# Loading attention's keys on 64 partitions instead of 128, and writing the low parts across

## The chip, the cores and the metric

One Trainium2 chip, one core. The metric is the device time of one execution in microseconds. The profile comes from one execution of its own.

## What is computed

Attention over 4 batches, 8 heads, 576 positions of 64 elements, with a mask by blocks of 64; its output is cut into 2304 tokens of 512, which pass a mixture of four experts and then a last layer with a softmax in it.

```python
scores = scale * np.matmul(q, k.transpose(0, 1, 3, 2))
mask = block_i >= block_j                       # blocks of 64 positions
scores = np.where(mask, scores, -1000000000.0)
attn = softmax(scores)
x = np.matmul(attn, v)                          # as (2304, 512)
for e in range(4):
    out += p[:, e:e + 1] * (np.maximum(x @ w1[e], 0.0) @ w2[e])
h = out @ w_in                                  # then softmax, a layer norm, @ w_out
```

## The kernel before

Tokens go in 18 tiles of 128 (TILES). Three things run woven into each other: attention in 60-odd steps (`step_a` the scores, `step_b` the exponentials, `step_c` the product with the values, `finish` the scaling of the result), the experts (`emit_h`, `emit_o`) for tiles whose attention is done, and the preparation of weights (`w_steps`). After attention the second half of the tokens goes through the last expert phases, and then the last layer (`m2_h`, `m2_o`).

**Products in parts.** A float32 value x is held as a high part, x rounded, and a low part, x less the high part. For the scores the contraction has 64 elements and TensorE has 128 rows, so the keys' tile `ks` holds the high part in partitions 0 to 63 and the low part in 64 to 127. The queries' tiles `qhi` and `qlo` hold their part twice, in both halves. One matmul of `qhi` and one of `qlo` with `ks` (L915, L918) so give all four products.

**How the keys got there.** The input `kT` has the same 64 rows twice, on 128 partitions. `k_load` and `k_far_load` (through `dup`, L781) load all 128 into a tile of the pool `kr`, which has three buffers and holds raw values (`vraw`) too. `parts` (L788) rounds all 128 partitions into `ks` (L793, on POOL in mode "pp") and then, on partitions 64 to 127 alone, writes raw less rounded over it in place (L795). Batch 0 is done in two pieces: `k_near` takes 192 columns from the tile `near`, and the far 384 columns of each of the eight heads come through `k_far_load`. Batches 1 to 3 take 576 columns for each head through `k_load` and `k_prep`, 24 in all.

**Other names.** `wt` is a split weight: POOL (L231) or ACT (L235) writes its high part, DVE (L238) its low part, in four pieces. `stage` is the raw weight. The first expert's w1 and w2 go through POOL. `hl` is a tile of exponentials in two parts; a DMA transpose on SP makes `pT` of it, on which `step_c` waits. `xh` is a tile of attention's result in two parts; a DMA transpose makes `xT`, on which the first expert matmul (`hps`, L375) waits. `hch` is the hidden layer, `ops` the expert's output.

**What sets the order.** All DMAs are issued by SP in one order, each when what it waits for is there, and a later one does not pass it. Every engine runs its instructions in a fixed order, which a scheduler works out ahead of the run from the program and its own estimate of each instruction's time; an edit to one instruction can so move others. The plan's step numbers (`plan`, L1082) say at which attention step a key is prepared, and up to three loads of the pool `kr` are issued ahead.

Of the kernel before, what the change touches and what calls it, by code (L numbers as in the profile page):

```python
# [7 lines left out]
F32 = mybir.dt.float32  # L8
# [6 lines left out]
AF = mybir.ActivationFunctionType  # L15
ALU = mybir.AluOpType
# [3 lines left out]
NB, NH, S, HD = 4, 8, 576, 64  # L20
# [10 lines left out]
NEAR = 192  # L31
# [32 lines left out]
def tile_kernel(  # L64
# [38 lines left out]
    vec, act, gp, sync = nc.vector, nc.scalar, nc.gpsimd, InOrder(nc.sync)  # L103
# [640 lines left out]
    class Attention:  # L744
# [43 lines left out]
        def parts(self, hi, lo, raw, ps, mode):  # L788
# [5 lines left out]
            eng = vec if mode[1] == "d" else gp  # L794
            eng.tensor_tensor(out=lo[ps], in0=raw[ps], in1=hi[ps], op=ALU.subtract)  # L795

        def k_load(self, b, h):
            self.raws["k", b, h] = self.dup([S], kT[:, b, h, :], "kr")

        def k_prep(self, b, h, mode="pp"):  # L800
            ks = self.kp.tile([128, S], F32R, tag="ks", name="ks")
            self.kS[b, h] = ks
            self.parts(ks, ks, self.raws.pop(("k", b, h)), slice(64, 128), mode)

        def k_near(self, p):

# [7 lines left out]

        def k_far_load(self, h):
            c = 0 if h % 2 == 0 else NEAR
            self.raws["far", h] = self.dup([S - NEAR], kT[:, 0, h, c:c + S - NEAR], "kr")

        def k_far(self, h, mode="pp"):
            c = 0 if h % 2 == 0 else NEAR  # L820
            o = self.kS[0, h][:, c:c + S - NEAR]
            self.parts(o, o, self.raws.pop(("far", h)), slice(64, 128), mode)

        def q_load(self, t, c):
            self.raws["q", t, c] = self.dup([4, 128], qT[:, t, 4 * c:4 * c + 4], "qr")
# [428 lines left out]
    def norm():  # L1254
# [12 lines left out]
        S=[lambda: at1.v_square(z0, 0, keep=True), lambda: at1.v_scale(z0, 1), lambda: at1.v_split(z0, 0)],  # L1267
# [107 lines left out]
    while at1.more:  # L1375
        t, u, cost = moe[-1] if moe else (-1, None, 0)
        ok = t is None or t in ready and len(bg) <= n1
        if not ok or tdv <= tpe + 2.0:
            flush()
            at1.step()  # L1380
            a, c = at1.cost()
# [233 lines left out]
```

## Time and profile before

| | us |
|---|---|
| median of 3 runs | 1094.97 |
| lowest, highest | 1093.44, 1098.03 |
| the profiled execution | 1094.33 |
| its span | 1092.5 |
| busy: PE, DVE, ACT, POOL | 1042.0, 786.2, 511.2, 182.9 |
| DMA: moved, packets | 137.95 MB, 225744 |

The span runs from the first to the last instruction; 1.8 us lie around it. Attention, and with it all work on keys, ends by 485 us; POOL is idle from there on. In the 40 slices of the page, PE is below 90% busy only in the first few, that is in the first 137 us and hardly after. So the rows that matter are those of the first 137 us, by stretch, by waiting engine, and by queue.

### The profile page before, as it was taken

The numbers are of one execution on the slowest core, as the hardware profiler recorded it, in microseconds if no ns is written. First come the engines' busy times: TensorE is split into PE (matmuls) and PEld (weight loads), VectorE is DVE, ScalarE is ACT, GpSimd is POOL, SyncE is SP. The second block draws the span as 40 slices with busy tenths as digits, with TensorE's granted clock in tenths as the row PEclk, the third lists the DMA queues.
The fourth block names the chain that finished last, engine by engine and source line by source line (L and its number), as shares of the span: only waits on it lengthen the run. The fifth ranks groups of instructions, "written<-read, shape, count | busy, mean of one in ns | idle before, by whom it ended". The sixth has DMA issues, their size and how long they took to land.

```text
span 1092.5 us, 20576 instructions
## 1 busy us (share of the span) xinstructions
PE 1042.0 (95%) x8088; PEld 656.8 (60%) x8088; DVE 786.2 (72%) x1758; ACT 511.2 (47%) x1108; POOL 182.9 (17%) x176
## 2 busy tenths in 40 slices
PE   4579899999999999999899999999999999999998
PEld 4556666556556655655576777766666674444444
DVE  6879787758758765545877556665879558999883
ACT  5767569546755554442453334231446353323322
POOL 4965633433125411000000000000000000000000
PEclk9989999999999999999999999999999999999999
DMA  9977997575887756326331212330245312434233
GB/s 292 274 168 162 242 194 185 151 181 139 184 180 180 159 123 130 71 46 191 102 107 54 78 49 69 116 136 30 97 145 153 90 20 34 92 87 101 64 87 87
DMA packets 225744, 137.95 MB, mean 126 GB/s; under 512 B 184560, under 2 KB 193008, under 8 KB 225648
## 3 DMA queue, kind: packets, MB, share of 16 engines
q1 hardware_dynamic: 225648, 136.65, 50.8%
q8 instruction: 63, 1.03, 0.4%
q14 instruction: 33, 0.27, 0.1%
HBM read 79.47 MB, written 12.06 MB: 84 GB/s over the span
## 4 chain that ended last, share of the span: by engine, by line
PE 78%; DVE 9%; DMA 6%; POOL 3%; issue 2%; ACT 2%; SPq 1%; DVEq 0%; ACTq 0%; POOLq 0%
PE ops L397 30%; PE hps L629 14%; PE hps L375 11%; PE o L1531 9%; PE h L1465 9%; PE pv L1016 2%; DMA pT<-hl 2%; DVE wt L238 2%; PE sps L915 2%; DVE hl L988 2%; PE sps L918 1%; SPq L94 1%; DVE v L877 1%; DMA stage<-in_w_dram 1%; DMA xT<-xh 1%
## 5 line engine op out<-in xcount | busy, mean ns | idle before, releaser
L397 PE MATMUL ops<-wt,hch 128*128 128x512 f16 x1728 | 393.4, 379 | 2.2 <-DVE wt L238 1.4
L397 PEld LDWEIGHTS <-hch 128*128 128x128 f16 x1728 | 165.9, 98 | 187.0 <-issue 6.5
L375 PE MATMUL hps<-xT,wt 128*128 128x384 f16 (+1 forms) x1536 | 216.7, 290 | 8.9 <-DVE hch L386 5.0
L375 PEld LDWEIGHTS <-wt 128*128 128x128 f16 x1536 | 126.6, 100 | 67.7 <-issue 9.3
L974 ACT ACTIVATE p<-sps,nm 128x320 f32<-128x320 f32 (+3 forms) x120 | 70.1, 587 | 92.3 <-DVE nm L934 76.9
L988 DVE TENSOR_TENSOR hl<-p,hl 128x320 f16<-128x320 f32 (+3 forms) x120 | 80.7, 689 | 33.9 <-ACT hl L987 33.5
L629 PEld LDWEIGHTS <-S 128*128 128x128 f16 x1152 | 96.0, 98 | 3.0 <-issue 0.9
L1531 PE MATMUL o<-wt,lt 128*128 128x512 f16 (+1 forms) x456 | 95.6, 368 | 0.0
L1465 PE MATMUL h<-wt,x2T 128*128 128x512 f16 x432 | 95.5, 379 | 0.0
L238 DVE SCALAR_TENSOR_TENSOR wt<-stage,ws,wt 128x1024 f16<-128x1024 f32 (+1 forms) x64 | 85.1, 1337 | 6.4 <-ACT wt L235 2.9
L422 DVE SCALAR_TENSOR_TENSOR acc<-ops,coef,acc 128x512 f32<-128x512 f32 x54 | 40.4, 749 | 68.2 <-PE ops L397 68.0
L915 PE MATMUL sps<-ks,qhi 128*128 128x288 f32 (+3 forms) x160 | 69.3, 434 | 12.6 <-DVE hl L988 6.7
L629 PE MATMUL hps<-T,S 128*128 128x192 f16 x864 | 76.3, 246 | 0.0
L629 PEld LDWEIGHTS <-wt 128*128 128x128 f16 x864 | 72.8, 98 | 5.8
L642 ACT ACTIVATE stu<-hps 128x384 f32<-128x384 f32 x72 | 34.6, 482 | 87.6 <-PE hps L629 87.4
L1531 PEld LDWEIGHTS <-lt 128*128 128x128 f16 x456 | 44.6, 98 | 48.9
L1465 PEld LDWEIGHTS <-x2T 128*128 128x128 f16 x432 | 42.3, 98 | 51.0
L386 DVE SCALAR_TENSOR_TENSOR hch<-hps,hch 128x384 f16<-128x384 f32 (+1 forms) x98 | 52.8, 540 | 22.1 <-ACT hch L385 22.1
L647 ACT ACTIVATE hch<-stc 128x384 f16<-128x384 f32 x72 | 37.4, 521 | 63.1 <-DVE stc L655 62.7
L385 ACT ACTIVATE hch<-hps 128x384 f16<-128x384 f32 (+1 forms) x98 | 46.9, 480 | 39.9 <-PE hps L375 39.7
L235 ACT ACTIVATE wt<-stage,ws 128x1024 f16<-128x1024 f32 (+1 forms) x56 | 60.2, 1096 | 4.0 <-DVE ws L143 4.0
L987 ACT ACTIVATE hl<-p 128x320 f16<-128x320 f32 (+3 forms) x120 | 60.2, 532 | 3.4 <-DMA pT<-hl 2.8
(163 smaller groups left out, 1497.6 us busy)
## 6 DMA issues: line engine op xcount, KB each, us to landing
stage<-in_w_dram SPq DMA_DIRECT2D x50, 512.0 KB, 6.0
raw<-in_qT_dram SPq DMA_DIRECT2D x34, 256.0 KB, 3.3
vraw<-in_vC_dram SPq DMA_DIRECT2D x30, 256.0 KB, 3.2
raw<-in_kT_dram SPq DMA_DIRECT2D x24, 288.0 KB, 3.6
raw<-in_w_dram SPq DMA_DIRECT2D x24, 256.0 KB, 3.7
raw<-in_w_in_dram SPq DMA_DIRECT2D x8, 512.0 KB, 4.9
raw<-in_w_out_dram SPq DMA_DIRECT2D x8, 512.0 KB, 4.2
stage<-wf SPq DMA_DIRECT2D x8, 512.0 KB, 6.3
```

Source lines behind the costliest of these rows:

```text
L235: h = paced_a(bg_(act.activation(out=hi, in_=r, func=AF.Copy, scale=stage[key, "s"]), "A"))
L238: stage["last"] = vec.scalar_tensor_tensor(out=lo, in0=r, scalar=stage[key, "s"], in1=hi, op0=ALU.mult, op1=ALU.subtract)
L375: pe.matmul(ps[:, j * n:j * n + n], w[:, a, kk, f * 128:(f + 1) * 128], x[:, b * KD + kk, c0:c0 + n], start=(m == 0), stop=(m == 3 * KD - 1),)
L386: marks["D"] = nc.vector.scalar_tensor_tensor(out=h[:, 1, :n], in0=ps[:, :n], scalar=0.0, in1=h[:, 0, :n], op0=ALU.max, op1=ALU.subtract)
L397: pe.matmul(ps, hch[f][:, a, o0:o0 + 128], w[:, b, f, :], start=(m == 0), stop=(m == 3 * KF - 1))
L629: i = pe.matmul(ps[x][:, jj * HT:jj * HT + HT], lhs(a, kk, jj), rhs(b, kk), start=start, stop=(m == 5), skip_group_check=not first or jj > 0,)
L915: pe.matmul(o, q, rhs, start=True, stop=False)
L974: act.activation(out=src if direct else dst, in_=src, func=AF.Exp, bias=nm[:, j + x:j + x + 1], scale=SCALE, accum_out=sums[:, h:h + 1],)
L987: anc["A"] = act.activation(out=hi, in_=pf, func=AF.Copy)
L988: anc["D"] = vec.tensor_tensor(out=lo, in0=pf, in1=hi, op=ALU.subtract)
L1465: pe.matmul(ps[:, half], x[:, a * KD + kk, c:c + 128], w[:, b, kk, half * 512:half * 512 + 512], start=(m == 0), stop=(m == 3 * KD - 1),)
L1531: pe.matmul(ps, tt[:, x * KF + f], w[:, y, f, c], start=(m == 0), stop=(m == 3 * KF - 1))
```

## The change

Keys other than the near ones of batch 0 and the `kZ` tiles are loaded once, 64 rows on partitions 0 to 63. The high part is rounded on these 64 partitions alone. The low part is read from partitions 0 to 63 (raw and high) and written to 64 to 127. The tiles, their pools and their number of buffers are the same, and so is what lies in `ks` when it is done.

```diff
+        def half(self, shape, src):
+            r = self.kr.tile([128, *shape], F32, tag="kr", name="raw")
+            sync.dma_start(out=r[0:64], in_=src[0:64])
+            return r
+
+        def k_parts(self, o, raw, mode):
+            a, b = slice(0, 64), slice(64, 128)
+            if mode[0] == "a":
+                act.activation(out=o[a], in_=raw[a], func=AF.Copy)
+            else:
+                gp.tensor_scalar(out=o[a], in0=raw[a], scalar1=1.0, scalar2=1.0, op0=ALU.mult, op1=ALU.mult)
+            (vec if mode[1] == "d" else gp).tensor_tensor(out=o[b], in0=raw[a], in1=o[a], op=ALU.subtract)
+
         def k_load(self, b, h):
-            self.raws["k", b, h] = self.dup([S], kT[:, b, h, :], "kr")
+            self.raws["k", b, h] = self.half([S], kT[:, b, h, :])
...
-            self.parts(ks, ks, self.raws.pop(("k", b, h)), slice(64, 128), mode)
+            self.k_parts(ks, self.raws.pop(("k", b, h)), mode)
...
-            self.raws["far", h] = self.dup([S - NEAR], kT[:, 0, h, c:c + S - NEAR], "kr")
+            self.raws["far", h] = self.half([S - NEAR], kT[:, 0, h, c:c + S - NEAR])
...
-            self.parts(o, o, self.raws.pop(("far", h)), slice(64, 128), mode)
+            self.k_parts(o, self.raws.pop(("far", h)), mode)
```

The number of instructions on every engine is the same; their order is not. (The new functions move the lines behind them by 14; L808 and L809 are the new splits.) Three places follow.

POOL, before, in the first attention steps: the last near key, a value tile, the high parts of the first w1 (`wt_415`), and only then the first far keys.

```order
L793 TENSOR_SCALAR ks_443<-near_156 128x192
L876 TENSOR_SCALAR v_277<-qv_137,vs_257 128x512
L231 TENSOR_SCALAR wt_415<-stage_205,ws_207 128x1024 x2
L793 TENSOR_SCALAR qhi_430<-raw_309 128x512
L231 TENSOR_SCALAR wt_415<-stage_205,ws_207 128x1024
L795 TENSOR_TENSOR qlo_431<-raw_309,qhi_430 128x512
L793 TENSOR_SCALAR qhi_582<-raw_578 128x512
...
L793 TENSOR_SCALAR ks_396<-raw_588 128x384
```

POOL, now, at the same place.

```order
L793 TENSOR_SCALAR ks_443<-near_156 128x192
L808 TENSOR_SCALAR ks_396<-raw_588 64x384
L808 TENSOR_SCALAR ks_399<-raw_590 64x384
L890 TENSOR_SCALAR v_277<-qv_137,vs_257 128x512
L808 TENSOR_SCALAR ks_424<-raw_592 64x384
L809 TENSOR_TENSOR ks_396<-raw_588,ks_396 64x384
L809 TENSOR_TENSOR ks_399<-raw_590,ks_399 64x384
L809 TENSOR_TENSOR ks_424<-raw_592,ks_424 64x384
L231 TENSOR_SCALAR wt_415<-stage_205,ws_207 128x1024 x3
```

Three far keys' high and low parts moved ahead of the four pieces of w1.

POOL, before, around the pieces of the first w2 (`wt_560`).

```order
L231 TENSOR_SCALAR wt_560<-stage_268,ws_270 128x1024
L795 TENSOR_TENSOR ks_437<-raw_642,ks_437 64x384
L231 TENSOR_SCALAR wt_560<-stage_268,ws_270 128x1024
L793 TENSOR_SCALAR ks_440<-raw_646 128x384
L793 TENSOR_SCALAR qhi_927<-raw_586 128x512
L793 TENSOR_SCALAR ks_443<-raw_771 128x384
```

POOL, now, at the same place.

```order
L808 TENSOR_SCALAR ks_440<-raw_646 64x384
L809 TENSOR_TENSOR ks_440<-raw_646,ks_440 64x384
L231 TENSOR_SCALAR wt_560<-stage_268,ws_270 128x1024
L808 TENSOR_SCALAR ks_443<-raw_771 64x384
L231 TENSOR_SCALAR wt_560<-stage_268,ws_270 128x1024
L809 TENSOR_TENSOR ks_443<-raw_771,ks_443 64x384
L231 TENSOR_SCALAR wt_560<-stage_268,ws_270 128x1024 x2
```

The last two far keys (`ks_440`, `ks_443`) moved from behind the last piece of w2 to ahead of it.

SP's queue, before, at the first transpose of finished tokens (`xT_477` from `xh_392`).

```order
L94 DMA_TRANSPOSE pT_376<-hl_369 128x8x128
L94 DMA stage_268<-in_w2_dram 128x2x512 x3
L94 DMA stage_1112<-in_w1_dram 128x1024 x2
L94 DMA_TRANSPOSE xT_477<-xh_392 128x8x128
L94 DMA_TRANSPOSE pT_517<-hl_510 128x6x128
L94 DMA raw_586<-in_qT_dram 128x512
```

SP's queue, now, at the same place.

```order
L94 DMA_TRANSPOSE pT_376<-hl_369 128x8x128
L94 DMA stage_268<-in_w2_dram 128x2x512 x3
L94 DMA stage_1112<-in_w1_dram 128x1024 x4
L94 DMA raw_586<-in_qT_dram 128x512
L94 DMA raw_646<-in_kT_dram 64x384
L94 DMA_TRANSPOSE xT_477<-xh_392 128x8x128
```

Two more loads of the next w1 (`stage_1112`), one of queries and one of keys moved ahead of the transpose.

## Rows read from the trace of the kernel before

**Rows 1.** The page, section 1: busy us, share of the span, instructions.

```profile
PE 1042.0 (95%) x8088; PEld 656.8 (60%) x8088; DVE 786.2 (72%) x1758; ACT 511.2 (47%) x1108; POOL 182.9 (17%) x176
```

**Rows 2.** Windows by stage: length, each engine's busy us, granted clock, DMA share, GB/s.

```profile
27.00:55.00 28.00, 16.29 (x176) 15.29 (x177) 24.59 (x59) 20.48 (x63) 26.07 (x24) 1.00 1.04 274
55.00:82.00 27.00, 20.47 (x217) 15.26 (x215) 21.15 (x41) 16.59 (x47) 17.76 (x16) 0.87 0.80 169
82.00:137.00 55.00, 49.43 (x652) 37.79 (x649) 46.17 (x90) 35.90 (x88) 34.08 (x29) 1.00 0.92 201
137.00:485.00 348.00, 342.79 (x2869) 206.97 (x2867) 236.45 (x499) 202.90 (x485) 93.08 (x87) 1.00 0.66 149
485.00:1092.00 607.00, 600.87 (x4123) 370.09 (x4120) 439.97 (x1021) 220.66 (x389) 0.00 (x0) 1.00 0.34 91
```

**Rows 3.** PE's timeline: start, length, work, in brackets its idle time before.

```profile
47.36 2.83 PE L375 MATMUL hps<-xT,wt 128*128 128x128 f16 x25 [1.58 <-DMA xT<-xh]
...
62.99 1.24 PE L397 MATMUL ops<-wt,hch 128*128 128x512 f16 x5 [0.94 <-DVE wt L238]
65.07 0.38 PE L397 MATMUL ops<-wt,hch 128*128 128x512 f16 x1 [0.83 <-POOL wt L231]
...
69.00 0.41 PE L915 MATMUL sps<-ks,qhi 128*128 128x320 f32 x1 [0.19 <-POOL ks L795]
71.55 0.41 PE L915 MATMUL sps<-ks,qhi 128*128 128x320 f32 x1 [1.56 <-POOL ks L795]
73.84 1.14 PE L1016 MATMUL pv<-v,pT 128*128 128x64 f16 x18 [1.46 <-DMA pT<-hl]
...
136.01 1.05 PE L1016 MATMUL pv<-v,pT 128*128 128x64 f16 x30 [1.38 <-DMA pT<-hl]
```

**Rows 4.** POOL's timeline, the same columns.

```profile
25.99 0.69 POOL L876 TENSOR_SCALAR v<-qv,vs 128x512 f16<-128x512 f32 x1 [2.21 <-DVE vs L143]
28.20 2.21 POOL L231 TENSOR_SCALAR wt<-stage,ws 128x1024 f16<-128x1024 f32 x2 [1.53 <-DVE ws L143]
...
63.90 1.12 POOL L231 TENSOR_SCALAR wt<-stage,ws 128x1024 f16<-128x1024 f32 x1
```

**Rows 5.** POOL's groups by line and form: count, busy us, mean ns of one.

```profile
L795 POOL TENSOR_TENSOR qlo<-raw,qhi 128x512 fp32r<-128x512 f32 x32 | 43.7, 1365 | 4.3 <-PE sps L920 2.5
L795 POOL TENSOR_TENSOR ks<-raw,ks 64x576 fp32r<-64x576 f32 x24 | 39.9, 1663 | 2.0
...
L795 POOL TENSOR_TENSOR ks<-raw,ks 64x384 fp32r<-64x384 f32 x8 | 10.0, 1271 | 0.4
L793 POOL TENSOR_SCALAR ks<-raw 128x384 fp32r<-128x384 f32 x8 | 7.1, 896 | 0.0
```

**Rows 6.** The timeline of SP's queue: start, length of issue, DMA, how many.

```profile
24.18 2.47 SPq L94 DMA_DIRECT2D raw<-in_kT_dram  x3
...
40.88 1.23 SPq L94 DMA_TRANSPOSE xT<-xh  x1
...
47.14 1.53 SPq L94 DMA_DIRECT2D raw<-in_kT_dram  x3
```

**Rows 7.** DMA issues, KB each, us to landing: all; 930 to 975; 110 to 137.

```profile
raw<-in_kT_dram SPq DMA_DIRECT2D x24, 288.0 KB, 3.6
...
raw<-in_kT_dram SPq DMA_DIRECT2D x8, 192.0 KB, 3.4
...
out_dram<-o2s SPq DMA_DIRECT2D x4, 128.0 KB, 2.3
out_dram<-o2s SPq DMA_DIRECT2D x2, 256.0 KB, 2.0
...
raw<-in_kT_dram SPq DMA_DIRECT2D x3, 288.0 KB, 4.9
```

**Rows 8.** Windows of other stretches, columns as in rows 2.

```profile
74.00:78.00 4.00, 4.00 (x47) 4.00 (x46) 3.13 (x8) 3.52 (x11) 0.02 (x1) 0.50 1.14 301
...
110.00:137.00 27.00, 23.26 (x323) 18.68 (x321) 20.89 (x44) 15.40 (x42) 18.36 (x17) 1.00 1.09 246
```

## Prediction

> **What bounds the kernel now.** I read the page's busy line first, then the stretches, then who PE waits for in the first 140 us, and last the two queues that the change reorders, POOL's and SP's. PE is busy 1042.0 us of the 1092.5 us span [rows 1], so 50.5 us of PE idle time is all that a change off PE can give back, apart from the clock. The stretches say where it lies [rows 2]: from 137 us on PE stands idle for 5.2 us (348 less 342.79) and 6.1 us (607 less 600.87) in 955 us, and there a shorter key load is worth nothing. Between 27 and 137 us it stands idle for 11.7, 6.5 and 5.6 us. The reader should see in the same rows what is busy instead: from 27 to 55 us POOL works 26.07 of 28 us, DVE 24.59, and the DMA engines show a share of 1.04, which is all of them all the time; from 82 to 137 us the DMA share is 0.92. So the start is bound by POOL and DVE with the DMA rings full beside them. PE's own waits there name the steps [rows 3]: 1.58 us for the first transposed tokens at 47.36, 0.94 and 0.83 for parts of the first w2, 0.19 and 1.56 for keys that POOL has not split, 1.46 and 1.38 for a transposed pT. POOL itself runs nearly without a gap from 28.20 to about 65 us; its two gaps just before are 2.21 and 1.53 us [rows 4].
>
> **Fewer bytes.** The eight far loads shrink from 192 to 96 KB and the 24 loads of batches 1 to 3 from 288 to 144 KB [rows 7], 768 + 3456 KB or 4.3 MB in all. Most of that falls after 137 us, where nothing waits for it. Between 24 and 55 us six far loads, issued at 24.18 and 47.14 [rows 6], save 0.59 MB, which at 274 GB/s [rows 2] is 2.15 us of the DMA engines; but PE waits there once for a transfer, the tokens, and that is costed below, so I take 0 of it (bounds 0 and -2.15). In 110 to 137 us three loads save 0.44 MB, at 246 GB/s 1.8 us [rows 7, 8], on rings on which pT also travels; PE waits 1.38 us for pT at 136.01 [rows 3]. I take **-1.38**, bounds 0 and -1.8.
>
> Whether half the bytes go in half the time no load of this kernel shows, since all have 128 partitions. The nearest rows are stores [rows 7]: the four output halves of 64 partitions and 128 KB took 2.3 us to land, the two of 128 partitions and 256 KB took 2.0. Halving bytes by halving partitions bought nothing there, though each is one small transfer on an idle ring. [...]
>
> **The splits on POOL.** The high part is now rounded on 64 partitions instead of 128, and the low part is written from partitions 0 to 63 into 64 to 127. For the first, an instruction's time follows its length and not its partitions: the subtraction on 64 partitions and 384 elements takes 1271 ns, on 128 and 512 1365 ns, so more time per element on fewer partitions [rows 5]. I take 0; the lower bound is half the high part's 896 ns, eight times, -3.6 us of POOL before 73 us. For the write across halves the trace has no row. Bounds: the present 1271 ns, and twice that, 10.2 us for eight; I take the present price, since the instruction reads and writes as many elements as before. ACT and DVE split none of these keys, so they lose and gain no instruction.
>
> **The order on POOL.** The three first far keys are now split ahead of the first w1, and the last two pairs of high and low parts come ahead of the last parts of w2. Ahead of the last w2 part there stood six pairs and now stand eight, so it comes 2 x (0.896 + 1.271) = 4.33 us later [rows 5] less what the early splits fill of the gaps of 2.21 and 1.53 us [rows 4]: 0.6 us later. Against that the two waits of PE for keys, 0.19 + 1.56, go [rows 3], as all keys are now split before. Net **-1.15**; bounds -1.75 (the w2 part hidden behind DVE) and +2.6 (no gap filled).
>
> **The order on SP.** Three far loads now go out ahead of the first pT and the other three ahead of the w2 loads; before they stood at 24.18 and 47.14 us [rows 6]. The piece that speaks against the change is the first xT. It was issued at 40.88, behind two loads of the next w1, and PE started on it at 47.36 [rows 3, 6]. Now all four w1 loads, one of queries and one of keys stand ahead of it: two more of 512 KB, 256 KB and 96 KB, 1.41 MB, which at 274 GB/s is 5.1 us. PE's later waits in the chain can take up 0.94 + 0.83 + 1.46 = 3.2 us of that [rows 3]; the rest is **+1.9**, bounds 0 (the loads wait for their stage and leave the rings free) and +5.1. Issue costs on SP do not change, as the number of loads is the same.
>
> [...]
>
> **Sum.** -1.38 - 1.15 + 1.9 = -0.6 us against the profiled execution's 1094.33 (span 1092.5 and 1.8 around it): **1093.7 us**. That execution is 0.06% below the median of 1094.97. What this kernel's runs can tell from no change is about 0.5%, 5.5 us, so the forecast is no change.
>
> **Rivals.**
> - *Bytes count everywhere* (faster): both bounds of the loads hold, the keys' waits go, xT is no later and the fall of the clock is gone: -2.15 - 1.8 - 1.75 - 2.0 = -7.7, 1086.6 us. For it: the DMA share of 1.04 and 0.92 [rows 2]. Against: PE waits only 1.58 + 1.46 + 1.38 us for transfers in this stretch, and only one of its waits follows a key load.
> - *The half load takes as long as the whole* (no change): the store rows [rows 7] carried over to loads. Then -1.15 + 1.9 = +0.8, 1095.1 us. It is the mechanism by which the change would not do what it says, as the bytes fall but the ring time doesn't. For it: 2.3 us against 2.0. Against: those rows are mostly a fixed time. [...]
> - *xT behind the weights* (slower): the four w1 loads, of 2 MB, go ahead of the first xT, PE starts its first hps 5.1 us later, and DVE, which has hch in its fixed order, waits with it, so nothing is taken up: 1099.4. PE's idle time ahead of it grows by as much, and I add a second fall of the clock, 2.0 us: 1101.4. It decides as soon as PE's start on xT moves past 50.6 us (47.36 and the 3.2 us of later waits).
> - *Writes across halves are dear on POOL* (slower): eight low parts at twice 1271 ns put 10.2 us on the chain that POOL closes at 65 us, less the 3.2 us of waits: 1101 to 1105. Against: same elements, same instruction. It decides above about 1.7 us for 384 elements.
>
> **How the numbers follow.** Forecast 0.34; half load as long 0.24; bytes count 0.20; xT late 0.15; dear writes 0.07. The fine order of all engines changes with it, which can move any of them by some 2 us. The first two lie within 0.5%, but for 0.01 each way: faster 0.21, same 0.56, slower 0.23. The range reaches up to the slower xT case and down to the faster one, 1086.5 to 1101.5; about half of the faster case lies beyond it, a part of the late xT and most of the dear writes: 0.2 left out.
>
> **What would show it.** Right: in the changed profile kT loads of 96 and 144 KB land in about 3 us, the low parts on POOL stay near 1.27 and 1.66 us, PE shows no wait for POOL's ks before 75 us, the DMA share in 110 to 137 us is below 1.09, and PE idle time from 137 us on stays near 11 us. Wrong: a low part of 2 us or more; first hps after 51 us; a clock of 0.50 somewhere else or nowhere; PE idle time after 137 us changed by more than 4 us, which would mean that the reordering decides and not the keys.

## The result: slower by 0.86%

The changed kernel took 1104.31 us (median of five runs, 1103.14 to 1104.52) against 1093.44 us (the kernel before, five runs now), a ratio of 1.0086 with a 95% interval of 1.0068 to 1.0103. The forecast was 1093.7 us, no change, in a range up to 1101.5: the measured time lies beyond it. The profiled execution took 1103.14 us, its span is 1101.3.

The busy line of the page, which answers to [rows 1]:

```profile
PE 1044.6 (95%) x8088; PEld 656.6 (60%) x8088; DVE 791.2 (72%) x1758; ACT 511.9 (46%) x1108; POOL 174.6 (16%) x176
```

The stretches, with the columns of [rows 2]:

```profile
27.00:55.00 28.00, 12.62 (x124) 11.48 (x124) 21.86 (x51) 19.44 (x54) 27.55 (x26) 1.00 0.95 262
55.00:82.00 27.00, 22.44 (x259) 17.41 (x255) 22.27 (x43) 16.30 (x51) 12.45 (x11) 0.87 0.59 134
82.00:137.00 55.00, 49.10 (x609) 35.75 (x607) 42.83 (x88) 34.68 (x82) 25.81 (x24) 0.94 0.89 171
137.00:485.00 348.00, 339.27 (x2855) 205.72 (x2853) 241.65 (x498) 201.42 (x485) 95.09 (x92) 1.00 0.64 144
485.00:1101.00 616.00, 609.13 (x4193) 374.95 (x4191) 444.00 (x1028) 224.69 (x395) 0.00 (x0) 1.00 0.33 90
```

The span grew by 8.8 us. PE idle time (length less PE's busy time) grew by 3.7 us in 27 to 55, fell by 2.0 in 55 to 82, and grew by 0.3, 3.5 and 0.7 us in the last three: 6.3 us in all behind 27 us. The rest, 2.6 us, is PE's busy time, 1044.6 against 1042.0, with the same products in it. The clock was low in more places, which can account for it; no run separates that. The same columns for four short stretches:

```profile
62.00:66.00 4.00, 4.00 (x35) 3.55 (x35) 4.00 (x7) 1.33 (x5) 1.96 (x1) 0.50 0.83 183
91.00:95.00 4.00, 4.00 (x15) 1.62 (x14) 2.47 (x8) 2.32 (x5) 0.00 (x0) 0.57 0.46 83
124.00:128.00 4.00, 4.00 (x39) 2.00 (x39) 1.94 (x3) 2.19 (x5) 0.00 (x0) 0.66 0.92 203
350.00:354.00 4.00, 4.00 (x28) 2.34 (x27) 3.58 (x8) 1.41 (x4) 0.00 (x0) 0.57 0.53 133
```

Each stands right behind a wait of PE. Its timeline, as in [rows 3]:

```profile
45.08 0.50 PE L929 MATMUL sps<-ks,qhi 128*128 128x192 f32 x1 [6.80 <-DVE hl L1002]
...
51.23 2.67 PE L375 MATMUL hps<-xT,wt 128*128 128x128 f16 x25 [0.59 <-DMA xT<-xh]
...
61.60 0.61 PE L929 MATMUL sps<-ks,qhi 128*128 128x320 f32 x1 [4.22 <-DVE hl L1002]
...
89.48 0.70 PE L1030 MATMUL pv<-v,pT 128*128 128x64 f16 x18 [2.17 <-DMA pT<-hl]
...
123.90 1.05 PE L1030 MATMUL pv<-v,pT 128*128 128x64 f16 x30 [2.60 <-DMA pT<-hl]
...
349.49 3.01 PE L375 MATMUL hps<-xT,wt 128*128 128x384 f16 x12 [2.03 <-DVE hch L386]
```

What the change was about got no dearer. POOL's groups, as in [rows 5], and the key loads, as in [rows 7] (all of 144 and of 96 KB, then the three in 110 to 137 us):

```profile
L809 POOL TENSOR_TENSOR ks<-raw,ks 64x576 fp32r<-64x576 f32 x24 | 39.0, 1625 | 2.0
...
L808 POOL TENSOR_SCALAR ks<-raw 64x576 fp32r<-64x576 f32 x24 | 17.9, 746 | 75.2 <-PE sps L932 42.6 <-PE sps L934 21.2 <-DMA raw<-in_kT_dram 11.3
...
L809 POOL TENSOR_TENSOR ks<-raw,ks 64x384 fp32r<-64x384 f32 x8 | 9.4, 1187 | 0.3
...
L808 POOL TENSOR_SCALAR ks<-raw 64x384 fp32r<-64x384 f32 x8 | 4.0, 515 | 0.0
```

```profile
raw<-in_kT_dram SPq DMA_DIRECT2D x24, 144.0 KB, 3.0
...
raw<-in_kT_dram SPq DMA_DIRECT2D x8, 96.0 KB, 5.1
...
raw<-in_kT_dram SPq DMA_DIRECT2D x3, 144.0 KB, 3.1
```

So POOL worked 8.3 us less, and the loads of 144 KB landed in 3.0 us. The 96 KB loads took longer than the old ones of 192 KB (3.4) because of where they now go out, among the first weights: at the old order (x1 below) they landed in 2.9. The loss lies in waits for DVE and for pT.

### The profile page after: what moved, and what is told of

It reads as the page before. It is cut to its first block, busy times and chain, and to the rows that moved or that the text cites. A ratio compares the mean times of both kernels' runs of the same rounds, so it can differ in the third digit from the quotient of the medians.

```text
span 1101.3 us, 20572 instructions
## 1 busy us (share of the span) xinstructions
PE 1044.6 (95%) x8088; PEld 656.6 (60%) x8088; DVE 791.2 (72%) x1758; ACT 511.9 (46%) x1108; POOL 174.6 (16%) x176
## 4 chain that ended last, share of the span: by engine, by line
PE 80%; DVE 7%; DMA 6%; POOL 2%; issue 2%; ACT 2%; SPq 0%; DVEq 0%; POOLq 0%; ACTq 0%
PE ops L397 32%; PE hps L629 14%; PE hps L375 10%; PE o L1545 8%; PE h L1479 8%; DMA pT<-hl 3%; PE pv L1030 3%; PE sps L929 2%; PE sps L932 1%; DVE hl L1002 1%; DVE wt L238 1%; DVE v L891 1%; DVE hch L386 1%; DMA xT<-xh 1%; DMA x2T<-xh 1%
## 5 line engine op out<-in xcount | busy, mean ns | idle before, releaser
L1030 PE MATMUL pv<-v,pT 128*128 128x64 f16 x1392 | 56.1, 196 | 9.0 <-DMA pT<-hl 8.2
L1030 PEld LDWEIGHTS <-pT 128*128 128x128 f16 x1392 | 51.1, 100 | 18.6 <-DMA pT<-hl 10.7
```

The lines of the kernel that those rows point to most:

```text
L1030: pe.matmul(o, tt[:, a * nch + c, :], v[:, bb, hs], start=(m == 0), stop=(m == total - 1))
```

## The experiments

Single runs of one kernel lie up to 9 us apart (1090.8 to 1099.8 in 25 runs of the kernel before), the short ones mostly with the higher mean clock (0.998 down to 0.991), so all times are medians of 4 to 12 runs, with ratios to the kernel before on the same chip. Where a number is called clock loss, it is (1 less the mean granted clock) times the span, a mean over the runs: 5.6 us for the kernel before (25 runs), 8.6 for the changed one.

### The order, or the instructions

Two theories: the loss comes from the order in which the engines now run; or the half loads and the writes across cost something. The way to part them: record the names of each engine's instructions in one kernel's order, and chain them in that order in the other. The chain is by engine and adds no wait.

```diff
+def fix_order(tc):
+    for eng, names in STORED.items():
+        for a, b in zip(names, names[1:]):
+            tc.add_manual_dep(SEEN[b], SEEN[a], ...)
...
+    fix_order(tc)
```

**x1_new_work_old_order**: the changed kernel, STORED from the kernel before.

> The changed kernel's instructions (half loads, high parts on 64 partitions, low parts written across), with every engine held to the exact order of the kernel before. Theory (only the order costs): as the kernel before or a little faster, 1090 to 1095 us, first wait of PE for hl as before (no 6.8 us wait at 48 us), clock at 0.50 only near 74 to 78 us. Rival (the half loads or the writes across cost): 1102 to 1106 us, as the changed kernel.

**x2_old_work_new_order**: the kernel before, STORED from the changed one. It also lacks two lines of the old load function, as in e2 below, which would hold the early key loads back.

> The kernel before's instructions (whole loads, 128 partitions), with every engine held to the exact order of the changed kernel. Theory (only the order costs): 1101 to 1107 us, with waits of PE for hl of about 6.8 us near 48 and 4 us near 61 us and falls of the clock behind them. Rival (the half loads or the writes across cost): 1092 to 1096 us, as the kernel before.

**x0_old_work_old_order**: the kernel before with its own order, as the control.

> The kernel before itself with its own order held in the way of the other runs. It tells whether that way costs anything and whether the rows repeat: 1091 to 1096 us, pt 0.21 us, xh 0.74 us, no wait of 2 us near 345 us. If the time is above 1098 us, the comparisons with the held order have to be read against this run and not against the kernel before.

| | old order | new order |
|---|---|---|
| old instructions | x0: 1094.86, 0.9998 (0.9983 to 1.0013) | x2: 1100.79, 1.0054 (1.0034 to 1.0074) |
| new instructions | x1: 1095.67, 1.0017 (0.9996 to 1.0038) | changed: 1104.31, 1.0086 (1.0068 to 1.0103) |

The order alone costs 0.54%, with the new instructions 0.69. The new instructions cost 0.17% in the old order and 0.32 in the new one, which is at the edge of what the intervals resolve. Holding an order costs nothing. x1 and x2 lie 0.7 and 0.2 us outside the ranges of their theory, on the sides that leave the instructions a small share.

PE's waits for pT follow the order too: 4.6 us in the profile of the kernel before, 3.7 in x0 and 4.8 in x1, but 8.2 in the changed kernel and 10.6 in x2.

Where does the new order come from? The old load function, `dup` (L784, L785), puts the early loads behind a transpose of pT; the function that replaces it, `half`, lacks these two lines.

```diff
         def half(self, shape, src):
...
-            sync.dma_start(out=r[0:64], in_=src[0:64])
+            x = sync.dma_start(out=r[0:64], in_=src[0:64])
+            if self.n < 8 and "sync" in marks:
+                after(x, marks["sync"])
```

**e1_paced**: the changed kernel with them (the diff above).

> The changed kernel with the two lines that its new load function lost: early loads are ordered behind the first transpose of pT again. The scheduler works the order out anew from this. Theory (the lost pacing moved the order): 1090 to 1097 us, the first far keys again behind the first w1 on POOL. Rival (the half loads or the writes across cost): 1102 to 1106 us.

**e2_before_unpaced**: the kernel before, `dup` without them for keys (`if tag != "kr" and ...`).

> The kernel before with those two lines dropped for the key loads alone, the loads and splits left whole. The scheduler's order then comes close to that of the changed kernel. Theory (the lost pacing moved the order): 1100 to 1107 us. Rival (the half loads or the writes across cost): 1092 to 1097 us.

Dropping two lines in the old kernel costs 0.68% (0.44 to 0.92; 1100.38 us), about as much as the whole change. Putting them back does not undo it: 1.0051 (1.0033 to 1.0069), 1100.22 us, between the ranges of both theories. So these lines are not the only reason: with other loads and splits in its own estimate the scheduler still arrives at another order, and e2's order is not the changed kernel's either. Lacking the lines costs next to nothing at a held order, since x1 lacks them too. Three orders other than the old one (the changed kernel's, e1's and e2's) thus each come with 0.5 to 0.9% more; why the old one is better is not shown. e1's clock loss was 7.9 us.

### Which stretch of the order

The two orders differ up to about 200 us, and by one small swap near 310. In these kernels STORED is one order for what starts before a time T, and the other behind it (h2 and n105: the other way round); the instructions are the changed kernel's.

```diff
-STORED = {e: old[e] for e in engines}
+first = {a for a in start if start[a] < T}
+STORED = {e: [a for a in old[e] if a in first] + [a for a in new[e] if a not in first] for e in engines}
```

> The changed kernel's instructions. All five engines held to the order of the kernel before for what that kernel starts in its first 52 us, and to the changed kernel's order for all the rest. Theory (the loss is made in the first 52 us, where the first xT came 4.4 us later, and is carried to the end): 1096 to 1101 us, first xT issued by 43 us. Rival (the order further on, at the w2 pieces and in 80 to 150 us, makes it): 1102 to 1106 us.

> The counterpart: the changed kernel's instructions, all engines held to the changed kernel's order for what it starts in its first 56 us, and to the order of the kernel before for all the rest. Theory (the loss is made in the first 52 us): 1098 to 1103 us, first xT issued at about 45 us. Rival (the order further on makes it): 1093 to 1098 us.

h1 took 1105.35 us and h2 1097.85: the theory that the loss is made in the first 52 us, where hl comes late for the first time, fell. In h2 the first xT still went out 4.6 us late, and by 149 us 1.3 of them were left; waits further on took up the rest. Four more moved T.

> The changed kernel's instructions; all engines in the old order for what the kernel before starts in its first 80 us, in the new order behind. With the change of order at 0 us it took 1104.3, at 52 us 1105.4. If the stretch of 52 to 80 us (the w2 pieces and the wait for hl near 61 us) makes the loss: 1096 to 1099 us. If a later stretch does: 1102 to 1106 us.

> The same with the old order to 105 us. If 80 to 105 us (the pT waited for at 89 and 102 us) makes the loss: 1096 to 1099 us, while the one with 80 us stays at 1102 to 1106. If 105 to 160 us (pT behind the next w1 loads near 113 us) does: 1102 to 1106 us.

> The same with the old order to 160 us. The two orders differ hardly at all behind that, so 1094 to 1097 us, as with the old order throughout (1095.7). If it stays above 1100 us, the small rest of the order or the changed instructions make the loss, and the stretches don't.

> The counterpart: new order for what the changed kernel starts in its first 105 us, old behind. With the change at 56 us it took 1097.9. If 56 to 105 us makes the loss: 1102 to 1106 us. If 105 to 160 us does: 1096 to 1099 us.

| T | old, then new | new, then old |
|---|---|---|
| 0 / none | 1.0086 | 1.0017 |
| 52, 56 | 1.0088 (1.0058 to 1.0118) | 1.0025 (1.0008 to 1.0042) |
| 80 | 1.0033 (1.0018 to 1.0048) | |
| 105 | 1.0051 (1.0032 to 1.0069) | 1.0052 (1.0033 to 1.0070) |
| 160 | 1.0019 (1.0001 to 1.0036) | |
| all | 1.0017 | 1.0086 |

Both columns give the same split, as differences of ratios in their points: up to 52 us -0.0002 and +0.0008, 52 to 105 us 0.0037 and 0.0027, behind 105 us 0.0034 and 0.0034. So the loss of some 7 us is about two halves, one in 52 to 105 us and one in 105 to 160, and next to nothing in the stretch with the longest wait. Each such difference is uncertain by some 0.003, so the halves are rough; that g105 and n105 lie between the ranges of their two theories fits them. (g80 and g105 stand in the wrong order by 0.0018, within their intervals, so the middle is not cut finer.)

Two runs asked which engine: the old order up to 52 us on POOL alone (s2) or on DVE and ACT alone (s3), the new one on the others.

> The changed kernel's instructions in the changed kernel's order on PE, DVE, ACT and SP; POOL alone held to the old order for the first 52 us, so the far keys' splits come behind the first w1 again. Theory A (POOL's order is the root: w1's parts come 1 to 3 us later and the rest waits for them): 1097 to 1101 us. Theory B (DVE's order is the root: exponentials' parts stand behind a low part of w1 and behind values): 1101 to 1106 us, DVE still waiting at the same places.

> The counterpart: DVE and ACT held to the old order for the first 52 us, PE, POOL and SP in the changed kernel's. Theory A (POOL's order is the root): 1101 to 1106 us. Theory B (DVE's order is the root): 1097 to 1101 us, the 6.8 us wait of PE for hl near 45 us gone or below 4 us.

With POOL alone (s2) 1115.14 us, 1.0186: worse than either order, and outside both theories. DVE and ACT alone (s3): 1099.84, 1.0055 (1.0038 to 1.0071), with PE's wait for hl down from 6.8 to 3.59 us, as theory B had it. But all five engines together (h1) gained nothing in the same stretch, so B is not borne out as the root of the loss either. A part of an order taken on one engine alone says little here. Other mixtures by engine were not tried.

### The waits for pT

The trace suggested a mechanism for the two later places. SP's queue in the changed kernel at 109 us:

```profile
109.72 2.66 SPq L94 DMA_DIRECT2D stage<-in_w_dram  x4
112.48 0.42 SPq L94 DMA_DIRECT2D vraw<-in_vC_dram  x1
113.01 7.40 SPq L94 DMA_TRANSPOSE pT<-hl  x1
```

Four weight loads go out ahead of a transpose, whose issue alone then takes 7.40 us. PE reaches its product with the values and stands 2.60 us at 123.90, and only then runs the twelve expert products that follow. The long issue is not new. The kernel before has it too:

```profile
113.10 1.96 SPq L94 DMA_DIRECT2D stage<-in_w_dram  x3
...
116.84 6.30 SPq L94 DMA_TRANSPOSE pT<-hl  x1
```

Yet PE there waits for no pT between 107 and 136 us, since it has other work until then. So what can differ is the work that covers the flight. In f1 the two groups that wait in the changed kernel go behind the expert products on PE:

```diff
-  pv x18 (89.48), sps x6, ops x5
+  sps x6, ops x5, pv x18
...
-  pv x30 (123.90), ops x12
+  ops x12, pv x30
```

> The changed kernel in its own order, but for two groups of products with the values on PE that waited there for pT (2.17 us at 89.48 and 2.60 us at 123.90): each is put behind the expert products that follow it (5 and 12 of them), and on DVE the xf that reads the first group goes behind the next maximum. Theory (the new order puts products with the values ahead of the work that used to cover pT's flight): both waits under 1 us, the falls of the clock behind them gone, 1096 to 1100 us. Rival (the rings or DVE are the bound there and the order only shows it): the waits come back at the next group, 1102 to 1106 us.

It took 1102.98 us, 1.0082 (1.0057 to 1.0107): nothing gained. Both waits are gone from their places and others have come:

```profile
77.31 0.70 PE L77 MATMUL pv<-v,pT 128*128 128x64 f16 x18 [2.87 <-DVE hl L77]
...
100.99 0.87 PE L77 MATMUL pv<-v,pT 128*128 128x64 f16 x24 [2.60 <-DMA pT<-hl]
...
134.33 1.78 PE L77 MATMUL pv<-v,pT 128*128 128x64 f16 x30 [2.61 <-DMA pT<-hl]
```

The rival's expectation came true: move a group on PE alone, and PE waits as long for a later one. Which of the moves in 52 to 160 us would have to be undone stays open.

### What the new instructions do at the same order

In every profile of the new splits PE stands idle for 2.5 to 3.1 us in 300 to 400 us, in the kernel before, x0, x2 and e2 for 0.7 to 0.9; the difference is the wait near 345 us. Behind it stands DVE's xh near 331 us: 0.74 us before, 1.88 in x1. From there DVE runs nearly without a gap to the hch that PE waits for, which starts 10.5 us after xh in the kernel before and 13.0 in x1; two low parts of weights in between are longer as well. POOL's qlo beside xh: 1.77 before, 1.26 in x1. f2 is x1 with DVE's xh ahead of a small copy:

```diff
-  vt<-vtp, xh<-xf,xs,xh
+  xh<-xf,xs,xh, vt<-vtp
```

> The changed kernel's instructions in the order of the kernel before, but that on DVE near 331 us the low part of xh (128x512) goes ahead of a copy of one column (0.15 us) instead of behind it. Theory (POOL's qlo started 0.02 to 0.09 us before DVE's xh there and the later of the two ran after the earlier): xh about 0.74 us instead of 1.88, qlo about 1.77 instead of 1.26, PE's wait of 2.03 us for hch near 345 us gone, 1091 to 1094 us. Rival (the 2 us near 345 come from the shorter high parts or the loads themselves): the wait stays, 1094 to 1097 us.

> The changed kernel in its own order with both edits: the two groups behind the expert products, and xh ahead of the copy near 335 us. If both theories hold, the gains add: 1093 to 1098 us. If neither does: 1102 to 1106 us.

f2: 1095.30 us, 1.0010 (0.9994 to 1.0026), the wait of 2.03 us still there at 345.90; f3 (the swap and f1's edit) 1102.31, 1.0079 (1.0054 to 1.0105). The premise of f2 was a misreading: xh had started ahead of qlo already, by 0.09 us before and by 0.07 in x1. In f2 it started 0.14 us ahead, while the high part before qlo still ran, and still took 1.94 us:

```profile
332.19 1.94 DVE L77 SCALAR_TENSOR_TENSOR xh<-xf,xs,xh 128x512 f16<-128x512 f32 x1
...
331.70 0.66 POOL L77 TENSOR_SCALAR ks<-raw 64x576 fp32r<-64x576 f32 x1
332.33 1.25 POOL L77 TENSOR_TENSOR qlo<-raw,qhi 128x512 fp32r<-128x512 f32 x1
```

So the start against qlo does not decide it. Two kernels in the old order with whole loads of 128 partitions, so that the loads are out of it:

```diff
-            sync.dma_start(out=r[0:64], in_=src[0:64])
+            sync.dma_start(out=r, in_=src)
```

> The kernel before's order with its whole loads on 128 partitions, but the changed kernel's splits: high part on 64 partitions, low part written across. It tells the loads from the splits in what is left at the same order. If the half loads move POOL ahead of DVE near 331 us: xh about 0.74 us, no wait of 2 us near 345 us, 1092 to 1095 us. If the splits do: xh 1.88 us and the wait of 2.03 us are there, 1094 to 1098 us.

x5 has this and the high part on 128 partitions again, so that only the write across is new (and, as in x1 and x3, the two lines of `dup` are missing):

```diff
-                gp.tensor_scalar(out=o[a], in0=raw[a], ...)
+                gp.tensor_scalar(out=o, in0=raw, ...)
```

> The kernel before's order and whole loads, the high part rounded on 128 partitions again, and only the low part written across from partitions 0 to 63. If the high part on 64 partitions makes DVE wait: pt about 0.21 us near 38 us, xh about 0.74 near 331 us, no wait of 2 us near 345 us, as in the kernel before. If the write across does: 1.10, 1.89 and 2.03 us, as with the changed splits. The time, 1092 to 1097 us, can hardly tell them apart; the rows do.

x3 took 1095.26 us, 1.0012 (0.9996 to 1.0028), x5 1094.30, 0.9992 (0.9975 to 1.0009). The rows tell them apart. The timeline of the kernel before from 37 us, first DVE, then POOL, then PE's wait for hl:

```profile
38.26 0.21 DVE L1074 TENSOR_SCALAR pt<-pn,xi 128x4 f32<-128x4 f32 x1
...
38.65 1.29 DVE L238 SCALAR_TENSOR_TENSOR wt<-stage,ws,wt 128x1024 f16<-128x1024 f32 x1
...
39.93 0.92 DVE L1070 SCALAR_TENSOR_TENSOR xh<-xf,xs,xh 128x512 f16<-128x512 f32 x1
...
36.92 3.39 POOL L793 TENSOR_SCALAR ks<-raw 128x384 fp32r<-128x384 f32 x3
40.28 1.69 POOL L795 TENSOR_TENSOR qlo<-raw,qhi 128x512 fp32r<-128x512 f32 x1
42.05 2.91 POOL L795 TENSOR_TENSOR ks<-raw,ks 64x384 fp32r<-64x384 f32 x3
...
41.59 0.50 PE L915 MATMUL sps<-ks,qhi 128*128 128x192 f32 x1 [2.19 <-DVE hl L988]
```

x3, the same instructions (everything ahead of them is 0.17 us later and equally long):

```profile
38.43 1.10 DVE L77 TENSOR_SCALAR pt<-pn,xi 128x4 f32<-128x4 f32 x1
...
39.71 2.11 DVE L77 SCALAR_TENSOR_TENSOR wt<-stage,ws,wt 128x1024 f16<-128x1024 f32 x1
...
41.81 1.41 DVE L77 SCALAR_TENSOR_TENSOR xh<-xf,xs,xh 128x512 f16<-128x512 f32 x1
...
37.09 2.42 POOL L77 TENSOR_SCALAR ks<-raw 64x384 fp32r<-64x384 f32 x3
39.48 1.25 POOL L77 TENSOR_TENSOR qlo<-raw,qhi 128x512 fp32r<-128x512 f32 x1
40.81 4.21 POOL L77 TENSOR_TENSOR ks<-raw,ks 64x384 fp32r<-64x384 f32 x3
...
43.96 0.50 PE L77 MATMUL sps<-ks,qhi 128*128 128x192 f32 x1 [4.40 <-DVE hl L77]
```

x5, whose highs are on 128 partitions:

```profile
37.69 0.21 DVE L77 TENSOR_SCALAR pt<-pn,xi 128x4 f32<-128x4 f32 x1
...
38.08 1.29 DVE L77 SCALAR_TENSOR_TENSOR wt<-stage,ws,wt 128x1024 f16<-128x1024 f32 x1
...
39.36 0.92 DVE L77 SCALAR_TENSOR_TENSOR xh<-xf,xs,xh 128x512 f16<-128x512 f32 x1
...
36.35 3.39 POOL L77 TENSOR_SCALAR ks<-raw 128x384 fp32r<-128x384 f32 x3
39.71 1.69 POOL L77 TENSOR_TENSOR qlo<-raw,qhi 128x512 fp32r<-128x512 f32 x1
41.49 2.91 POOL L77 TENSOR_TENSOR ks<-raw,ks 64x384 fp32r<-64x384 f32 x3
...
41.02 0.50 PE L77 MATMUL sps<-ks,qhi 128*128 128x192 f32 x1 [2.20 <-DVE hl L77]
```

The reader should see that at this place POOL's instructions get shorter and DVE's longer. With highs on 128 partitions POOL takes 3.39 us for three and DVE's pt takes 0.21; with highs on 64 POOL needs 2.42 and DVE's pt ends only as the third high does, at 39.5. POOL saves 1.4 us on these four instructions and DVE loses 2.2 on its three (0.9 + 0.8 + 0.5). POOL's saving does not last: its three low parts behind take 4.21 us instead of 2.91. PE's wait for hl grows from 2.19 us to 4.40. The control x0 repeats the old rows (0.21, 1.29, 0.92; 3.39, 1.69, 2.91), and so does x5. So the write across is innocent, and so are the half loads, since x3 has none; it is the high part on 64 partitions.

PE's waits for hl in all are 9.4 us in the kernel before, 8.3 in x0 and x5, and 14.5 and 15.2 in x1 and x3. At the old order the time takes that nearly without loss, since other waits give way: those for xT are 4.5 us in x0 and 1.9 in x1. Over the first 520 us, which hold all work on keys, POOL's busy time falls from 182.9 to 176.3 us in x1 and DVE's rises from 366.0 to 373.0; x3 and x5, at 371.9 and 371.6, are not told apart by DVE's sum.

Near 331 us xh grows by about what qlo beside it runs: by 1.14 us in x1, with a qlo of 1.26. Which of the two starts first does not decide whose time is the long one. In f2, x3 and x5 xh started first, by 0.14, 0.07 and 0.10 us. Where the high part ahead of qlo was on 64 partitions (f2, x3), xh took 1.94 and 1.89 us and qlo 1.25 and 1.26; where it was on 128 (x5), xh took 0.74 and qlo 1.77. Why, no run shows.

## Why the prediction was wrong

**The bound** was read rightly in part: it was DVE and transfers of pT that PE waited for. But of the 6.3 us of PE idle time that came on top, 4.3 lie behind 137 us, where the prediction looked for nothing.

**Fewer bytes, -1.38.** The order moves the landing as much as the size does, so it is read at one order (median of the 24 loads in us, in brackets the three in 110 to 137 us):

| | old order | new order |
|---|---|---|
| 288 KB on 128 partitions | x3: 3.8 (4.8) | x2: 3.5 (3.5) |
| 144 KB on 64 partitions | x1: 3.3 (5.7) | changed: 3.0 (3.1) |

Half a load landed 0.5 us sooner, far from in half the time, and in 110 to 137 us it landed later at one order and sooner at the other. So the rival by which it takes as long as a whole one was nearly right about the loads. Against it stood that the stores' rows are mostly a fixed time; in the trace of the kernel before the bytes of the 256 KB store issued at 955.79 moved from 956.6 to 957.4, 0.8 of its 2.0 us, at 328 GB/s, and those of the two halves of 128 KB issued at 939.29 from 940.4 to 941.8, at 193 GB/s. At the old order x1 and x3 took 1.0017 and 1.0012, so no gain shows, though 1.4 us would drown in intervals of 2 us. PE's waits for pT, which the saved bytes were to shorten, were 4.8 us in x1 and 3.4 in x3.

**The splits on POOL, 0.** The price of the write across was right: 1269 ns in x5 against 1271, and 0.9992 in time, so the rival with dear writes is out. In the changed kernel the low parts took 1187 and 1625 ns. The step that failed here is that a saving on POOL was taken as POOL's own affair. The rounding on 64 partitions is hardly shorter by itself (515 and 746 ns; 519 and 770 on 128 in x2, at the same order). Where it got shorter, at the old order (626 ns for 384 elements in x1, 899 in x0), DVE's instructions beside it got longer, pt, wt and xh together by 2.2 us in x3.

**The order on POOL, -1.15, and on SP, +1.9.** Here the forecast failed. Both terms took the new order as a few moves and priced each by the waits that it touched, +0.75 us in sum. As a whole it costs 0.54 to 0.69%, 6 to 7 us. In the first 56 us, where the moved splits and the first xT lie, next to nothing of it is made. xT went out 4.4 us later and the first hps at 51.23, past the 50.6 us that the prediction named; but the rival built on that, 1101.4 us, had the wrong reason. The weights ahead on the rings cost xT nothing: from its issue to PE's start on it 5.9 us passed, and 6.5 before. It was issued late, 3.0 of the 4.4 us because DVE's xh ended at 43.87 instead of 40.85, the rest behind a key load that SP issued only at 44.76. And in h2 the delay was mostly taken up later. The moves around the w2 pieces lie in the stretch of 52 to 105 us, which costs 3 to 4 us; their term was +0.6 with a bound of +2.6. The stretch behind 105 us, as dear, had no term for its order. The prediction had a sentence that the fine order could move any case by some 2 us; it was the largest term of all, and had no row and no chance of its own. One source of a new order, the two lines that the new function no longer has, stood in the code and was overlooked. Which moves make the loss stays open.

**The clock.** The forecast counts nothing for it. The 2.0 us that two rivals count for a fall are an estimate, half of the 4 us at a clock of 0.50 [rows 8]; no run shows what a fall costs by itself. Even so it is too little: the clock of 0.87 over 27 us [rows 2], taken in the same way, is 3.5 us. The changed kernel has falls at 62, 91, 124 and 350 us in the profiled execution in place of one at 74, the last behind the wait that belongs to the splits, and its clock loss over the runs is 3.0 us larger (8.6 less 5.6). The order alone does not bring that: x2 and e2 lose 5.8 and 4.0 us by the clock, and yet 0.54 and 0.68% in time. In x2's profile PE stands idle 5.6 us longer than before (56.1 against 50.5).

**What would show it.** One line of that list gave the right answer, by luck: PE's idle time behind 137 us changed from 11.3 to 15.6 us (8.73 + 6.87), by more than the 4 us that were to mean that the reordering decides and not the keys. Of the 4.3 us, 1.9 stand in 137 to 160 us, 1.7 in 300 to 400 and 0.7 behind 485; the second part belongs to the splits, not to the order, and without it the sign would have failed. Also right were the low parts' prices, the DMA share in 110 to 137 us (1.04), and that PE no longer waits for POOL's ks ahead of 75 us; wrong was a landing of about 3 us for the loads of 96 KB. The first hps after 51 us and a clock of 0.50 in another place stood there as signs of being wrong, and both came.

## What to carry to other kernels

A change that lets a scheduler place instructions anew has the price of a new order as a term of its own, and no list of the moved instructions gives it; hold the old order and change the work, hold the work and change the order, and the two prices fall apart in two runs. Compare the ordering constraints of a replaced function line by line, as its dependencies are part of what it did. And where an instruction on one engine gets shorter, others beside it on another can get longer, as with POOL's 1.4 us and DVE's 2.2 in x3: look at both engines' durations, not only at the changed one's.

## What was not expected of the hardware

- At two places of the old order the number of partitions of POOL's rounding (64 or 128, the same elements on each) decided whether POOL's or DVE's instructions took longer: DVE's pt 1.10 or 0.21 us beside three roundings in 2.42 or 3.39 us on POOL at otherwise equal rows (x3, x5), and xh 1.89 or 0.74 us beside a qlo of 1.26 or 1.77. It does not hold everywhere: in the new order pt took 1.36 us with highs on 64 and 0.41 on 128 (x2), while POOL took the same time, 1.45 and 1.46 us for three. POOL's own time does not follow the partitions: 515 ns on 64 in the changed kernel, 519 ns on 128 in x2, in the same order.
- Loads of 144 KB on 64 partitions landed in 3.0 us and of 288 KB on 128 in 3.5 at the same order (x2): half the bytes saved a seventh of the time. Whether a fixed time or the number of partitions is the reason is not shown.
- A subtraction that reads partitions 0 to 63 and writes 64 to 127 costs what one in place does (1269 ns in x5, 1271 before, for 384 elements).
